# Local attention and a two-matrix FFN on one core: the stationary of the FFN matmuls read with a step of four columns

## The chip, the cores and the metric

The kernel runs on one core of a Trainium2 chip. Its time is the time of one execution on the device, in microseconds (us); several executions are made and their median is given. The core's engines are TensorE (PE in the profile, with its loads of the stationary shown apart as PEld), VectorE (DVE), ScalarE (ACT), GpSimd (POOL) and SyncE (SP). In this kernel SP issues every transfer between DRAM and the chip's memory. A matmul on PE has a stationary operand, which is loaded by an instruction of its own, and a moving operand, which is streamed against it.

## The reference

The input is q, k and v for 4 batches of 8 heads, 768 tokens, 64 numbers per head, and 8 memory keys and values per head. Attention is local: tokens go in chunks of 32, and a chunk sees the memory, 16 tokens to its left, itself, and 8 to its right.

```python
for c in range(S // 32):
    k_full = concat([mem_k, k[:, :, max(0, 32*c - 16) : min(S, 32*c + 40)]])   # v_full likewise
    scores = q[:, :, 32*c : 32*c + 32] @ k_full.T / sqrt(64)
    a = exp(scores - max(scores)); a = a / (sum(a) + 1e-9)
    out[:, :, 32*c : 32*c + 32] = a @ v_full
x = out as 3072 tokens x 512
h = x @ w_in                                # 512 -> 2048
g = where(h >= 1, h, where(h <= -1, 0, (h + 1)**2 / 4))
result = g @ w_out                          # 2048 -> 512
```

## The kernel before

The 3072 tokens are six blocks of `TB = 512` tokens (`NB = 6`), and the FFN's 2048 hidden numbers are `NFC = 16` slices of 128. A step `s` is one slice `fc` of one block `blk`. In each step PE makes the hidden slice and then, two steps later (`LAG`), adds its share of the output. Both weights and both activations are split into a high and a low part (`wh`, `wl`; `xh`, `xl`; `gh`, `gl`) of type fp32r, and three of the four products are summed.

*Hidden product* (`pe_hidden`, and the same lines in `early_step`). The stationary is a 128-column piece of the weight slice, one for each of the `NP = 4` groups of 128 input channels; the moving operand is x, 512 tokens wide. The weight slice of one `fc` lies in a partition as 512 words, group after group, so piece `cc` is the 128 words from `cc * P`. Three products by four groups are 12 matmuls.

*Output product* (`pe_products`). Here the stationary is a piece of the gated activation, 128 tokens, and the moving operand is the row of w_out, 512 columns wide. A block has `NT = 4` token tiles, tile `t` being the 128 tokens from `t * P`. Three products by four tiles are again 12 matmuls. Their sums stay in PSUM over all 16 slices (`acc`), one bank for a tile.

*Gating*. ACT and DVE turn the hidden slice into `gh` and `gl`. *Store*: after the last slice of a block each tile's sum is copied by DVE or ACT and written by SP into 128 consecutive rows of `out`, one row (2 KB) per partition.

*The beginning.* Blocks 0 and 1 are done by the list `FIRST`, an order written out by hand in which each name is one piece of work: `g` and `n` are attention, `w` the decoding of a weight transfer by DVE and ACT, `A`, `B`, `C`, `D` are FFN steps over half a block (256 tokens, two token tiles; A and B the halves of block 0, C and D those of block 1, slices 0 to 3 each), and `J`, `E` are FFN steps over the whole of block 0 or 1. A half step's hidden matmuls have 256 moving columns. In it `pe_products` gets two tiles only, and `g` is the half's own 256 tokens.

*The rest.* From `s = first * NFC` with `first = 2` on, a loop runs the steps of blocks 2 to 5, with the attention of later blocks spread between them. All instructions are kept in the program's order on each engine.

The weights come in 16 transfers of 1 MB, packed in 64 bits per weight, in the order that `weight_order` gives; `_lay_out` arranges all inputs before the program runs.

Of the kernel before, what the change touches and what calls it, by code (L numbers as in the profile page):

```python
# [16 lines left out]
P = 128  # L17
CHUNK, LEFT, RIGHT = 32, 16, 8
TB = 512
NCH = TB // CHUNK  # L20
NT = TB // P
# [47 lines left out]
def attn_ffn_kernel(ctx: ExitStack, tc: tile.TileContext, first_qk, first_v, qk, vw, w, out):  # L69
    nc = tc.nc  # L70
    engines = (nc.tensor, nc.scalar, nc.vector, nc.gpsimd, nc.sync)
    pe, act, dve, pool, sp = (InOrder(tc, e) for e in engines)
    NP = first_qk.shape[0]
# [3 lines left out]
    DM = NP * P  # L77
    NPW = w.shape[0]
    NFC = NPW
# [14 lines left out]
    def two_banks(tag, name):  # L94
        return ps_2.tile([P, 2, 512], F32, name=name, tag=tag)
# [43 lines left out]
    def weights(which, fc, part):  # L139
        i, j = place[which, fc]  # L140
        c0 = part * n2 + j * DM
        return ws[i][:, c0 : c0 + DM]
# [248 lines left out]
    gate, gs, acc, hidden = {}, {}, {}, {}  # L391

    def hidden_terms(wh, wl, xh, xl):
        return [(m, x, cc) for m, x in ((wh, xh), (wl, xh), (wh, xl)) for cc in range(NP)]

    def pe_products(outs, gh, gl, wh, wl, fc):

        kinds = list(enumerate(((gh, wh), (gh, wl), (gl, wh))))
        todo = [(t, kind) for kind in kinds for t in range(len(outs))]
        if fc == NFC - 1:  # L400
            todo.sort(key=lambda x: x[0])
        for t, (i, (g, m)) in todo:
            ts = slice(t * P, (t + 1) * P)
            pe.matmul(outs[t], g[:, ts], m, start=fc == 0 and i == 0, stop=fc == NFC - 1 and i == 2)

    def pe_hidden(s):
        blk, fc = divmod(s, NFC)
        xh, xl = xts[blk]
        hp = hidden[s] = ps_h.tile([P, 512], F32, name="ps_h")
        wh, wl = weights(0, fc, 0), weights(0, fc, 1)  # L410
        terms = hidden_terms(wh, wl, xh, xl)
        for n, (m, x, cc) in enumerate(terms):
            pe.matmul(hp, m[:, cc * P : (cc + 1) * P], x[:, cc], start=n == 0, stop=n == len(terms) - 1)

    def gating(s):

# [24 lines left out]
    def pe_out(s):  # L441
        blk, fc = divmod(s, NFC)
        gh, gl = gs.pop(s)
        if fc == 0:
            pairs = [two_banks(f"a{i}", "ps_o") for i in range(NT // 2)]
            acc[blk] = [pairs[t // 2][:, t % 2] for t in range(NT)]
        wh, wl = weights(1, fc, 0), weights(1, fc, 1)
        pe_products(acc[blk], gh, gl, wh, wl, fc)

    items, halves = [], []  # L450

    def early_step(name, blk, tokens, fc):

        items.append(name)
        size = len(tokens) * P
        xh, xl = (x[:, :, tokens[0] * P : tokens[0] * P + size] for x in xts[blk])
        n = 0
        if size < TB:
            n = len(halves) % 2
            halves.append(name)  # L460
        hp = ps_h.tile([P, 512], F32, name="ps_h")[:, 0:size]
        wh, wl = weights(0, fc, 0), weights(0, fc, 1)
        terms = hidden_terms(wh, wl, xh, xl)
        for i, (m, x, cc) in enumerate(terms):
            pe.matmul(hp, m[:, cc * P : (cc + 1) * P], x[:, cc], start=i == 0, stop=i == len(terms) - 1)
        yield
        if n == 0:
            tiles = (
                gpool.tile([P, TB], F32, name="gw", tag="gw"),
                gpool.tile([P, TB], F32, name="gt"),  # L470
                gpool.tile([P, TB], F32R, name="gh", bufs=3),
                gpool.tile([P, TB], F32R, name="gl", bufs=3),
            )
            if size < TB:
                both["g"] = tiles
        else:
            tiles = both["g"]
        g, t, gh, gl = (x[:, n * HT : n * HT + size] for x in tiles)
        act.activation(g, hp, AF.Relu, bias=0.5, scale=0.5)
        act.activation(t, hp, AF.Relu, bias=-1.0)  # L480
        act.activation(g, g, AF.Square)
        yield
        dve.scalar_tensor_tensor(g, g, 1.0, t, op0=ALU.min, op1=ALU.add)
        yield
        act.copy(gh, g)
        yield
        dve.tensor_tensor(gl, g, gh.bitcast(F32), op=ALU.subtract)
        yield
        if fc == 0:
            acc.setdefault(blk, [None] * NT)  # L490
            pair = two_banks(f"a{tokens[0] // 2}", "ps_o")
            for t in tokens:
                acc[blk][t] = pair[:, t % 2]
        wh, wl = weights(1, fc, 0), weights(1, fc, 1)
        pe_products([acc[blk][t] for t in tokens], gh, gl, wh, wl, fc)
        yield
        if fc < NFC - 1:
            return
        for t in tokens:
            if t % 2 == 0:  # L500
                ob = apool.tile([P, 2, DM], F32, name="ob", tag="f", bufs=2)
            (act.copy if t % 2 else dve.tensor_copy)(ob[:, t % 2], acc[blk][t])
            r0 = blk * TB + t * P
            sp.dma_start(out[r0 : r0 + P, :], ob[:, t % 2])
            yield

    def store(blk):
        for t in range(NT):
            src = acc[blk][t]
            if t % 2 == 0:  # L510
                ob = apool.tile([P, 2, DM], F32, name="ob", tag="f", bufs=2)
            dst = ob[:, t % 2]
            if t == NT - 1:
                dve.tensor_copy(dst[:, 0 : DM // 2], src[:, 0 : DM // 2])
                act.copy(dst[:, DM // 2 : DM], src[:, DM // 2 : DM])
            elif t % 2:
                act.copy(dst, src)
            else:
                dve.tensor_copy(dst, src)
            r0 = blk * TB + t * P  # L520
            sp.dma_start(out[r0 : r0 + P, :], dst)

    def keep_warm(n):

# [27 lines left out]
    for name in FIRST.split():  # L552
# [4 lines left out]
        if name not in chains:  # L557
            kind, i = name[0], int(name[1:])
# [2 lines left out]


    begin = {}
    first = 2
    for blk in range(first + 1, NB):
        for half in range(2):
            begin[(blk - 1) * NFC + STARTS[half]] = (blk, half)
# [6 lines left out]
    for s in range(first * NFC, steps):  # L574
# [30 lines left out]
        else:  # L605
            n, i = LAST // LAG, s - first * NFC
# [6 lines left out]
    for s in range(steps - LAG, steps):  # L613
        pe_out(s)
    store(NB - 1)


def weight_order(n):

    order = [(0, 0), (0, 1)]  # L620
    for fc in range(2, n):
        order += [(0, fc), (1, fc - 2)]
    return order + [(1, n - 2), (1, n - 1)]
# [5 lines left out]
def _lay_out(q, k, v, mem_k, mem_v, moe_w_in, moe_w_out):  # L629
    import numpy as _np  # L630

    B, H, S, D = q.shape
    NM, NC = mem_k.shape[2], S // CHUNK
    NP, W = H // 2, NM + LEFT + CHUNK + RIGHT
    NB = B * S // TB

    def windows(mem, a):

        pad = _np.pad(a, ((0, 0), (0, 0), (LEFT, RIGHT), (0, 0)))
        win = [  # L640
            _np.concatenate([mem, pad[:, :, c * CHUNK : (c + 1) * CHUNK + LEFT + RIGHT]], axis=2)
            for c in range(NC)
        ]
        return _np.stack(win, axis=1).reshape(B * NC, H, W, D)

    def transposed(a):

        return a.transpose(1, 3, 0, 2).reshape(NP, 2 * D, -1)


    qt = transposed(q).reshape(NP, 2 * D, NB * 2, TB // 2).transpose(2, 1, 0, 3)
    kw = windows(mem_k, k).reshape(NB * 2, NCH // 4, 2, NP, 2, 2, W // 2, D)

    k0 = kw.transpose(0, 4, 7, 3, 1, 2, 5, 6).reshape(NB * 2, 2 * D, NP, NCH // 2 * W)
    kw = _np.stack([kw[:, :, 0], kw[:, :, 1][..., ::-1, :, :]], axis=2)
    kw = kw.transpose(0, 4, 7, 3, 1, 2, 5, 6).reshape(NB * 2, 2 * D, NP, NCH // 2 * W)
    qk0 = _np.concatenate([qt, k0], axis=3)[0:2].reshape(2, 2 * D, 2, -1).transpose(0, 2, 1, 3)
    qk = _np.concatenate([qt, kw], axis=3).reshape(NB, 2, 2 * D, -1)[1:]
    vw = windows(mem_v, v).reshape(NB, NT, 4, NP, 2, W, D)

    v0 = vw[0].reshape(2, 2, 4, NP // 2, 2, 2, W, D).transpose(0, 3, 1, 6, 4, 2, 5, 7)

    v1 = vw[1:].reshape(NB - 1, 2, NT // 2, 2, 2, NP, 2, W, D).transpose(0, 1, 3, 7, 5, 2, 4, 6, 8)
    DM, DF = moe_w_in.shape
    n = DF // 128

    slices = (
        moe_w_in.reshape(DM // 128, 128, n, 128).transpose(2, 1, 0, 3).reshape(n, 128, DM),
        moe_w_out.reshape(n, 128, DM),
    )  # L670
    w = _np.stack([slices[which][fc] for which, fc in weight_order(n)])
    w = w.reshape(n, 2, 128, DM).transpose(0, 2, 1, 3).reshape(n, 128, 2 * DM)
    arrays = {

        "first_qk": qk0.reshape(NP, 2 * D, -1),
        "first_v": v0.reshape(NP, 2 * W, NCH * D),
        "qk": qk,
        "vw": v1.reshape(NB - 1, 2, 2 * W, -1),
        "w": _np.ascontiguousarray(w).view(_np.int64),
    }  # L680
    return {name: _np.ascontiguousarray(a) for name, a in arrays.items()}
# [23 lines left out]
```

## Time and profile before

| | |
|---|---|
| median of 3 executions | 599.97 us (599.84 to 600.01) |
| the profiled execution | 600.11 us |
| its span, first to last instruction | 598.3 us |
| granted TensorE clock, mean | 0.999 |
| instructions | 12265 |
| PE busy, share of the span | 582.7 us, 97%, 5496 matmuls |
| loads of the stationary (PEld) | 483.5 us, 81%, 5496 loads |
| DVE, ACT | 325.6 us (54%), 280.3 us (47%) |
| weights | 16 transfers of 1024 KB |
| stores | 24 of 256 KB, 2.0 us from issue to landing |

The profile is of one execution. A row of a timeline gives the start, the time until the last of its instructions ended, the engine, the source line, the operation with the tiles that it writes and reads, the shape and the number of instructions. Since every operation is recorded through one helper (`InOrder`), nearly all rows carry line 63, and the tiles tell them apart: `ps_h` is the hidden product, `ps_o` the output product, `ps_s` and `ps_x` the two products of attention; `xth` and `xtl` are the parts of x, `wr` the decoded weights, `gh` and `gl` the gated activation. A row of a group gives the number of instructions, their busy time, the mean duration of one in ns, and the time for which the engine was idle just before them with what ended it. A row of a window gives for each engine the busy time and the number of instructions in that stretch, then the granted clock, the share of the transfer engines' time, and GB/s.

### The profile page before, as it was taken

The numbers are of one execution on the slowest core, as the hardware profiler recorded it, in microseconds if no ns is written. First come the engines' busy times: TensorE is split into PE (matmuls) and PEld (weight loads), VectorE is DVE, ScalarE is ACT, GpSimd is POOL, SyncE is SP. The second block draws the span as 40 slices with busy tenths as digits, with TensorE's granted clock in tenths as the row PEclk, the third lists the DMA queues.
The fourth block names the chain that finished last, engine by engine and source line by source line (L and its number), as shares of the span: only waits on it lengthen the run. The fifth ranks groups of instructions, "written<-read, shape, count | busy, mean of one in ns | idle before, by whom it ended". The sixth has DMA issues, their size and how long they took to land.

```text
span 598.3 us, 12265 instructions
## 1 busy us (share of the span) xinstructions
PE 582.7 (97%) x5496; PEld 483.5 (81%) x5496; DVE 325.6 (54%) x466; ACT 280.3 (47%) x503; POOL 0.7 (0%) x6
## 2 busy tenths in 40 slices
PE   5899999999999999999999999999999999999996
PEld 2888888788888888888888888888888888888885
DVE  5999999986474224636423644623564632322222
ACT  2689864554435335444435443434443444543442
POOL 0000000000000000000000000000000000000000
PEclk9999999999999999999999999999999999999999
DMA  8999300424051004012101223200310000100001
GB/s 355 422 418 419 148 1 0 178 82 168 1 177 71 0 1 158 26 65 108 71 1 71 107 71 107 71 1 34 144 71 2 1 2 0 71 0 1 0 1 70
DMA packets 9844, 55.31 MB, mean 92 GB/s; under 512 B 1088, under 2 KB 1088, under 8 KB 5184
## 3 DMA queue, kind: packets, MB, share of 16 engines
q1 hardware_dynamic: 9792, 54.53, 23.6%
q8 instruction: 43, 0.70, 0.5%
q14 instruction: 9, 0.07, 0.0%
HBM read 48.23 MB, written 6.29 MB: 91 GB/s over the span
## 4 chain that ended last, share of the span: by engine, by line
PE 82%; DVE 15%; issue 2%; DMA 1%; ACT 0%; DVEq 0%; ACTq 0%
PE ps_o L63 38%; PE ps_h L63 38%; DVE f L63 6%; PE ps_x L63 3%; DVE wr L63 2%; PE ps_s L63 2%; DVE gw L63 1%; DVE gl L63 1%; DVE pr L63 1%; DVE den L63 1%; DMA qk<-in_first_qk_dram 1%; DVE pt L63 1%; DVE mx L63 1%; DVE xtl L63 0%; DVE rin L63 0%
## 5 line engine op out<-in xcount | busy, mean ns | idle before, releaser
L63 PE MATMUL ps_h<-xth,wr 128*128 128x512 f32 (+1 forms) x832 | 195.6, 377 | 1.1 <-DVE wr L63 1.1
L63 PE MATMUL ps_o<-wr,gh 128*128 128x512 f32 x768 | 194.7, 390 | 0.0
L63 PEld LDWEIGHTS ps_h<-xth,wr 128*128 128x128 f32 x832 | 149.0, 190 | 30.3 <-DVE wr L63 1.5
L63 PEld LDWEIGHTS ps_o<-wr,gh 128*128 128x128 f32 x768 | 143.3, 188 | 29.4
L63 DVE SCALAR_TENSOR_TENSOR gw<-gw,gt 128x512 f32<-128x512 f32 (+1 forms) x104 | 67.2, 649 | 164.9 <-ACT gw L63 164.6
L63 ACT ACTIVATE gw<-ps_h 128x512 f32<-128x512 f32 (+1 forms) x104 | 58.6, 563 | 159.0 <-PE ps_h L63 158.9
L63 PE MATMUL ps_o<-wr,gl 128*128 128x512 f32 x384 | 106.9, 389 | 0.0
L63 PE MATMUL ps_h<-xtl,wr 128*128 128x512 f32 (+1 forms) x416 | 104.8, 374 | 0.0
L63 DVE TENSOR_TENSOR gl<-gw,gh 128x512 fp32r<-128x512 f32 (+1 forms) x104 | 67.4, 649 | 65.8 <-ACT gh L63 65.7
L63 ACT CAST gh<-gw 128x512 fp32r<-128x512 f32 (+1 forms) x104 | 61.1, 590 | 69.9 <-DVE gw L63 69.9
L63 PEld LDWEIGHTS ps_h<-xtl,wr 128*128 128x128 f32 x416 | 75.3, 190 | 13.9
L63 PEld LDWEIGHTS ps_o<-wr,gl 128*128 128x128 f32 x384 | 72.1, 188 | 15.1
L63 ACT ACTIVATE gw<-gw 128x512 f32<-128x512 f32 (+1 forms) x104 | 62.4, 600 | 0.0
L63 ACT ACTIVATE gt<-ps_h 128x512 f32<-128x512 f32 (+1 forms) x104 | 58.3, 561 | 0.0
L63 DVE STREAM_TRANSPOSE pt<-pr 32x512 f32<-32x512 f32 (+1 forms) x60 | 41.2, 698 | 1.3
L63 DVE SCALAR_TENSOR_TENSOR f<-w,f 128x1024 uint32<-128x1024 uint32 x32 | 39.0, 1220 | 0.4
L63 ACT ACTIVATE pr<-pr 128x1024 f32<-128x1024 f32 (+1 forms) x14 | 13.1, 937 | 35.1 <-DVE pr L63 35.0
L63 PEld LDWEIGHTS ps_x<-pt,v 64*64 64x64 f32 x1536 | 25.1, 142 | 5.0 <-issue 3.3
L63 PE MATMUL ps_x<-pt,v 64*64 64x32 f32 x1536 | 26.6, 226 | 1.2 <-ACT pt L63 1.2
L63 ACT CAST xth<-ps_x 128x512 fp32r<-128x512 f32 x24 | 13.1, 591 | 20.6 <-PE ps_x L63 20.6
L63 ACT CAST wr<-f 128x1024 fp32r<-128x1024 f32 x16 | 16.8, 1051 | 11.7 <-DVE f L63 11.7
L63 PEld LDWEIGHTS ps_s<-qk 64*32 64x32 f32 x1536 | 17.1, 112 | 6.1 <-issue 3.1
(27 smaller groups left out, 182.6 us busy)
## 6 DMA issues: line engine op xcount, KB each, us to landing
w<-in_w_dram SPq DMA_DIRECT2D x16, 1024.0 KB, 19.8
qk<-in_qk_dram SPq DMA_DIRECT2D x10, 1536.0 KB, 6.5
v<-in_vw_dram SPq DMA_DIRECT2D x10, 1024.0 KB, 5.5
out_dram<-ob SPq DMA_DIRECT2D x24, 256.0 KB, 2.0
qk<-in_first_qk_dram SPq DMA_DIRECT2D x4, 768.0 KB, 8.7
v<-in_first_v_dram SPq DMA_DIRECT2D x4, 512.0 KB, 12.7
```

The lines of the kernel that those rows point to most:

```text
L63: return self.tc.keep_in_program_order(getattr(self.engine, name)(*args, **kwargs))
```

## The change

The stationary of both FFN products is read with a step. For the hidden product the words of a weight slice are laid out interleaved: word `4 * j + cc` of a partition is column `j` of group `cc`, and the piece for group `cc` is every fourth word. For the output product a token tile is every fourth token of its block (blocks 2 to 5), or every second token of its half block (blocks 0 and 1, whose early steps work on halves). A store writes the rows of `out` that belong to such a tile. The operands of each matmul of the hidden product are the same numbers as before; those of the output product are other groups of 128 tokens, with the same results for each token.

```diff
+    first = 2
+
+    def of_tile(blk, t):
+        n = NT // 2 if blk < first else NT
+        at = t // n * n * P + t % n
+        return slice(at, at + (P - 1) * n + 1, n)
+
+    def rows_of(blk, t):
+        return out[blk * TB : (blk + 1) * TB, :][of_tile(blk, t), :]
+
-    def pe_products(outs, gh, gl, wh, wl, fc):
+    def pe_products(outs, gh, gl, wh, wl, blk, fc):
...
-            ts = slice(t * P, (t + 1) * P)
-            pe.matmul(outs[t], g[:, ts], m, start=fc == 0 and i == 0, stop=fc == NFC - 1 and i == 2)
+            pe.matmul(outs[t], g[:, of_tile(blk, t)], m, start=fc == 0 and i == 0, stop=fc == NFC - 1 and i == 2)
...  (pe_hidden, and the same in early_step)
-            pe.matmul(hp, m[:, cc * P : (cc + 1) * P], x[:, cc], start=n == 0, stop=n == len(terms) - 1)
+            pe.matmul(hp, m[:, cc::NP], x[:, cc], start=n == 0, stop=n == len(terms) - 1)
...  (early_step; the same in store)
-            r0 = blk * TB + t * P
-            sp.dma_start(out[r0 : r0 + P, :], ob[:, t % 2])
+            sp.dma_start(rows_of(blk, t), ob[:, t % 2])
...  (_lay_out)
-        moe_w_in.reshape(DM // 128, 128, n, 128).transpose(2, 1, 0, 3).reshape(n, 128, DM),
+        moe_w_in.reshape(DM // 128, 128, n, 128).transpose(2, 1, 3, 0).reshape(n, 128, DM),
```

More of the change, by code (lines that the diff above doesn't have):

```diff
@@ L447, in pe_out @@
         wh, wl = weights(1, fc, 0), weights(1, fc, 1)
-        pe_products(acc[blk], gh, gl, wh, wl, fc)
+        pe_products(acc[blk], gh, gl, wh, wl, blk, fc)
     items, halves = [], []
@@ L464, in early_step @@
         for i, (m, x, cc) in enumerate(terms):
-            pe.matmul(hp, m[:, cc * P : (cc + 1) * P], x[:, cc], start=i == 0, stop=i == len(terms) - 1)
+            pe.matmul(hp, m[:, cc::NP], x[:, cc], start=i == 0, stop=i == len(terms) - 1)
         yield
@@ L494, in early_step @@
         wh, wl = weights(1, fc, 0), weights(1, fc, 1)
-        pe_products([acc[blk][t] for t in tokens], gh, gl, wh, wl, fc)
+        pe_products([acc[blk][t] for t in tokens], gh, gl, wh, wl, blk, fc)
         yield
@@ L519, in store @@
                 dve.tensor_copy(dst, src)
-            r0 = blk * TB + t * P
-            sp.dma_start(out[r0 : r0 + P, :], dst)
+            sp.dma_start(rows_of(blk, t), dst)
     def keep_warm(n):
@@ L563, in attn_ffn_kernel @@
     begin = {}
-    first = 2
     for blk in range(first + 1, NB):
```

## The prediction

> **What bounds the kernel now.** I read the page first: the busy line, the slices and the engines' shares of the chain that ended last.
>
> ```profile
> span 598.3 us, 12265 instructions
> PE 582.7 (97%) x5496; PEld 483.5 (81%) x5496; DVE 325.6 (54%) x466; ACT 280.3 (47%) x503; POOL 0.7 (0%) x6
> PE   5899999999999999999999999999999999999996
> DVE  5999999986474224636423644623564632322222
> PEclk9999999999999999999999999999999999999999
> PE 82%; DVE 15%; issue 2%; DMA 1%; ACT 0%; DVEq 0%; ACTq 0%
> ```
>
> TensorE (PE) carries the chain. VectorE (DVE) is full only in the first eight slices, some 110 us, where it decodes weights; afterwards it has room. The granted clock is full. A matmul's end in this trace is modelled, so a PE that is 97% busy can still have room. I therefore take start times from the timeline: first a step in the middle (24 matmuls of 512 moving columns, each with a stationary of its own), then a stretch with 256 moving columns, then the four transposes of an attention group (once a narrow view of the first, once all four).
>
> ```profile
> 300.33 1.77 PEld L63 LDWEIGHTS ps_h<-xth,wr 128*128 128x128 f32 x8
> 300.56 1.98 PE L63 MATMUL ps_h<-xth,wr 128*128 128x512 f32 x8
> 303.28 1.98 PE L63 MATMUL ps_o<-wr,gh 128*128 128x512 f32 x8
> ...
> 118.91 1.12 PE L63 MATMUL ps_h<-xth,wr 128*128 128x256 f32 x8
> 120.34 2.00 PE L63 MATMUL ps_o<-wr,gh 128*128 128x512 f32 x8
> ...
> 30.95 0.27 PE L63 MATMUL ps_h<-ident,pr 128*128 128x128 f32 x1
> 30.95 0.60 PE L63 MATMUL ps_h<-ident,pr 128*128 128x128 f32 x4
> ```
>
> From 300.56 to 303.28 lie twelve matmuls (eight of the high and four of the low part of x): 2.72 us / 12 = 227 ns each. From 118.91 to 120.34 lie twelve of 256 columns: 1.43 us / 12 = 119 ns each. The transposes: (0.60 - 0.27) / 3 = 110 ns from start to start. The first two differ by 108 ns for 256 columns, 0.42 ns a column, with 12 ns fixed: both follow the moving operand. At that pace 128 moving columns would take 66 ns. The transposes take 110, so something else limits them, and what is left there is the load of a 128-column stationary. **A load therefore holds its path for at most 110 ns**, although its own record is longer:
>
> ```profile
> L63 PEld LDWEIGHTS ps_h<-xth,wr 128*128 128x128 f32 x832 | 149.0, 190 | 30.3 <-DVE wr L63 1.5 <-issue 0.2
> L63 PEld LDWEIGHTS ps_o<-wr,gh 128*128 128x128 f32 x768 | 143.3, 188 | 29.4
> L63 PEld LDWEIGHTS ps_o<-wr,gl 128*128 128x128 f32 x384 | 72.1, 188 | 15.1
> L63 PEld LDWEIGHTS ps_h<-xtl,wr 128*128 128x128 f32 x416 | 75.3, 190 | 13.9
> 36.62 1.03 PEld L63 LDWEIGHTS ps_h<-xth,wr 128*128 128x128 f32 x8
> ```
>
> The last row has eight loads of 190 ns (1.52 us) in 1.03 us: records of following loads overlap, so 190 ns is a latency with a part that isn't occupancy. And the load of the next stationary runs beside the matmul before it: the row at 300.33 begins 0.23 us ahead of its matmuls. So there are two kinds of place. Under 512 moving columns a load may grow from 110 to about 227 ns, by a factor of 2.06, before anyone waits. Under 256 columns it has 119, 9 ns more than now.
>
> **The change part by part.** No instruction is added or removed. What changes is the address step of the stationary's columns, the order of the words in w_in and the rows of `out` that a store writes.
>
> Counts. Loads of the hidden product: 832 + 416 = 1248, all with a step of four (16 bytes of a partition). Loads of the output product: 768 + 384 = 1152; blocks 0 and 1 have 2 x 16 x 12 = 384 of them, with a step of two, and blocks 2 to 5 the other 768, with a step of four. Step four in all: 2016. Those of them that stand before a 256-column matmul are the half-token steps A, B, C and D:
>
> ```profile
> L63 PE MATMUL ps_h<-xth,wr 128*128 128x256 f32 x128 | 19.4, 297 | 0.0
> L63 PE MATMUL ps_h<-xtl,wr 128*128 128x256 f32 x64 | 10.7, 291 | 0.0
> 113.00:150.00 37.00, 37.00 (x484) 32.67 (x472) 29.88 (x47) 17.78 (x44) 0.00 (x0) 1.00 0.40 144
> 20.00:105.00 85.00, 82.15 (x817) 70.26 (x818) 84.13 (x113) 61.40 (x105) 0.00 (x0) 1.00 0.54 223
> 105.00:107.00 2.00, 1.05 (x4) 0.53 (x4) 2.00 (x2) 1.70 (x4) 0.00 (x0) 1.00 0.43 102
> ```
>
> 128 + 64 = 192, half of them (C and D, block 1) after 113 us, where PE is busy 37.00 of 37.00 us: any nanosecond there is on the path. The other half (A and B) lies in the first 50 us, where DVE has 84.13 of 85 us and PE still waits 2.85 us in this stretch and 0.95 us at 105; some of a delay there is swallowed, some pushes DVE, which waits for hidden results in its own order. I count half of it as exposed, 0 to all as the range. So 96 + 48 = 144 loads count (96 to 192).
>
> What a stepped load costs isn't in this trace: every PE operand in it is contiguous. The bounds come from the nearest rows.
>
> ```profile
> L63 DVE TENSOR_SCALAR f<-w 128x1024 uint32<-128x1024 uint32 x16 | 11.0, 687 | 0.0
> L63 DVE TENSOR_TENSOR gl<-gw,gh 128x512 fp32r<-128x512 f32 x88 | 60.8, 691 | 64.8 <-ACT gh L63 64.8
> L63 DVE TENSOR_TENSOR gl<-gw,gh 128x256 fp32r<-128x256 f32 x16 | 6.6, 418 | 1.0 <-ACT gh L63 0.9
> ```
>
> - Below: 110 ns, unchanged. A gain is excluded: under 512 and 256 columns the moving operand sets the pace, so a faster load would bring nothing.
> - DVE's decode reads every second word, 1024 words over 8192 bytes of a partition, in 687 ns with its fixed part, that is 16 bytes in 1.34 ns. It is quicker per word than the contiguous two-operand row (691 - 418 = 273 ns for 256 words), so nothing of a step shows in it. A load of step four has to walk 128 x 16 = 2048 bytes: at this pace 172 ns; without the fixed part (about 145 ns by the two rows of `gl`) 136 ns.
> - Above: PE's own moving operand walks 2048 contiguous bytes in 227 ns at most. A load that walked no faster would take 227 ns.
>
> All of these are at or under 227 ns, so in every 512-column step the longer load stays beside the matmul; the cover is the 227 ns itself, and past that each ns costs 1 ns on 2016 - 192 = 1824 loads, 1.8 us. Under 256 columns the cost per ns above 119 is 0.144 us (0.096 to 0.192): at 136 ns 2.4 us, at 172 ns 7.6 us, at 227 ns 15.6 us (10.4 to 20.7).
>
> I take the unchanged 110 ns, cost 0. It is the value of the load itself, and the only row with a stepped read shows no price for it; the load asks for one word per 0.85 ns, which is a slower demand than DVE's two words per 1.06 ns in that row.
>
> The Trainium skill speaks against this. Its page "SBUF — State Buffer", section "Specifications (TRN2)", gives lines of 16 bytes and wants at least two hits per line for full bandwidth; a step of four 4-byte words has one, a step of two has two. It names no price for a load; by it the 1248 + 768 loads of step four would get slower and the 384 of step two not, and the time would be that of the first rival below. DVE's row has two hits per line and agrees with the rule; no run here has shown one hit per line.
>
> The stores: 24 of 256 KB, as before one row of `out` (2 KB) per partition, only that rows that follow in a tile are four (blocks 0 and 1: two) apart in DRAM. The same pieces, so I take nothing; only the last four lie on the path, at the end:
>
> ```profile
> out_dram<-ob SPq DMA_DIRECT2D x24, 256.0 KB, 2.0
> 593.10 2.47 SPq L63 DMA_DIRECT2D out_dram<-ob  x4
> ```
>
> Bounds: their landing could move by some tenths of the 2.0 us, +-0.5 us. SP's queue holds the same issues in the same order; what waits behind a store there is the next block's loads, many us ahead of need. The x tiles, gating and attention are untouched, and w_in is rearranged outside the program, with the same 16 transfers.
>
> Sum: 0 under 512 columns, 0 under 256, 0 at the stores. The profiled execution took 600.11 us (span 598.3), 0.14 above the median of 599.97; so the forecast is 600.0.
>
> **The rivals.**
> 1. The stepped load gets slower, but not beyond 227 ns. Place: the 256-column steps alone. It decides from 119 ns on. For it: only 9 ns of room there, and PE without a gap after 113 us. Against: DVE's row. Taken at 172 ns, 600.0 + 7.6 = 607.6 us; from 601.6 (136 ns, C and D alone) to 620.7.
> 2. The load goes past 227 ns, or the two reads of PE get into each other's way by as much. It decides from a factor of 2.06. Against: no row near gives so slow a walk. Price 1.8 us per ns under 512 columns: at three times 110 ns, 330, it is 103 x 1.8 = 185 us, and 211 x 0.144 = 30 under 256: about 815 us.
> 3. The four stores of a block now interleave in DRAM. If the program orders them as overlapping, each waits for the landing of the one before: at the end, issues 2.0 us apart from 593.10, the fourth landing at 601.1 in place of about 597.2 (last issue 593.10 + 2.47 less its record of some 0.3, plus 2.0): +3.9, 603.9 us. Against: the rows are disjoint. For: their ranges are not.
> 4. Something outside this sum makes it faster, by placement or landing: 599.
>
> **How the numbers follow.** Chances: forecast 0.50; rival 1 0.33; rival 2 0.10; rival 3 0.04; rival 4 0.03. About 0.2% (1.2 us) is what a measurement of this kernel can tell from no change. The forecast gives "within" with 0.50; rivals 1 to 3 are slower by more than 0.2%, 0.47 in all; rival 4 gives faster, 0.03. Range: down to 599.2 for the landing of the stores; up to 614.0, which takes in rival 1 to a load of about 216 ns by the 144 count, and rival 3. Left out are rivals 2 and 4 and the top of rival 1, about 0.18. The likeliest alone has 599.4 to 600.6.
>
> **What would show it.** The four load groups in the costliest groups tell the step's own price: records near 190 mean no price, longer ones with the same start distances mean a hidden one. The distance of the 256-column starts is the judge: 119 ns for the forecast, 136 and more for rival 1, with the step at 113 us and the end later by the sum. The middle steps must keep 227 ns; more is rival 2. The loads of the output product in blocks 0 and 1 (step two) against those later (step four) show whether it is the step's width that counts. The last four stores must issue within 2.5 us; 2 us apart is rival 3. The forecast fails if the path of the load, unlike DVE's, can't take a new 16 bytes for every column at its pace.

## The result: 6.1% slower

The changed kernel takes 636.65 us (median of 4 executions, 636.53 to 636.73) against 599.95 us before: 36.7 us more, a ratio of 1.0612 with a 95% interval of 1.0593 to 1.063. The forecast was no change, with a range up to 614.0.

The page of the changed kernel, in the lines that answer to those of before:

```profile
span 634.9 us, 12265 instructions
PE 620.2 (98%) x5496; PEld 594.1 (94%) x5496; DVE 327.2 (52%) x466; ACT 281.6 (44%) x503; POOL 0.7 (0%) x6
PE   5899999999999999999999999999999999999996
PEclk9999999999999999999999999999999999999999
PE 96%; DVE 2%; DMA 1%; ACT 0%; issue 0%; DVEq 0%; ACTq 0%
L63 PEld LDWEIGHTS ps_h<-xth,wr 128*128 128x128 f32 x832 | 203.6, 313 | 2.6 <-issue 0.2
L63 PEld LDWEIGHTS ps_o<-wr,gh 128*128 128x128 f32 x768 | 175.0, 271 | 8.4
L63 PEld LDWEIGHTS ps_h<-xtl,wr 128*128 128x128 f32 x416 | 106.1, 313 | 0.0
L63 PEld LDWEIGHTS ps_o<-wr,gl 128*128 128x128 f32 x384 | 90.8, 271 | 5.1
out_dram<-ob SPq DMA_DIRECT2D x24, 256.0 KB, 2.2
```

The instructions are the same in number and the clock is full. DVE and ACT have the same work as before. What moved is PEld, 483.5 to 594.1 us: the mean load record of the hidden product went from 190 to 313 ns, that of the output product, a third of which has a step of two, from 188 to 271. PE, which had only 82% of the chain, now has 96%: DVE's 15% in the first 110 us is down to 2%, because PE has become the slower one there too. The timeline of a step in the middle and of a stretch with 256 moving columns, as in the prediction, and of an output product of block 0 (its step is two):

```profile
301.22 2.04 PE L63 MATMUL ps_h<-xth,wr 128*128 128x512 f32 x8
304.04 2.04 PE L63 MATMUL ps_o<-wr,gh 128*128 128x512 f32 x8
306.86 0.40 PE L63 MATMUL ps_h<-xth,wr 128*128 128x512 f32 x1
...
128.88 1.92 PE L63 MATMUL ps_h<-xth,wr 128*128 128x256 f32 x8
130.63 1.09 PE L63 MATMUL ps_h<-xtl,wr 128*128 128x256 f32 x4
131.57 2.02 PE L63 MATMUL ps_o<-wr,gh 128*128 128x512 f32 x8
...
71.44 2.03 PE L63 MATMUL ps_o<-wr,gh 128*128 128x512 f32 x8
73.30 1.10 PE L63 MATMUL ps_o<-wr,gl 128*128 128x512 f32 x4
```

Under 512 columns a step of 24 matmuls takes 306.86 - 301.22 = 5.64 us, 235 ns each, where it was 227. Under 256 columns the four matmuls of the low part take 0.94 us, 235 ns each (the most frequent distance in the trace is 233), where it was 119. And in block 0, with a step of two, eight starts take 1.86 us, 233 ns each. **So nearly every matmul of the FFN now starts 231 to 240 ns after the one before it, whether 256 or 512 columns stream.** The price by these distances: 192 x 113 ns (233 against 120, the most frequent distances in the two traces) = 21.7 us under 256 columns, 1824 x 8.2 = 15.0 us under 512 with a step of four, 384 x 6 = 2.3 us with a step of two. That is 39.0, and 36.7 were measured. Laid start against start, the two traces show the difference under 256 columns: what follows a 512-column matmul of the FFN grew by 17.3 us in all, as in the sum, but what follows a 256-column one by 19.3, of which 9.1 lie in the first 107 us. Before the change fifteen of those early starts already stood 213 ns apart, for a reason that the profile doesn't show, so they lost only 20 ns each:

```profile
25.73 1.05 PE L63 MATMUL ps_h<-xtl,wr 128*128 128x256 f32 x4
26.58 1.35 PE L63 MATMUL ps_h<-xth,wr 128*128 128x256 f32 x8
```

The last four stores of the changed kernel stand as before:

```profile
629.46 2.52 SPq L63 DMA_DIRECT2D out_dram<-ob  x4
```

### The profile page after: what moved, and what is told of

Read it like the earlier page. It is cut to its first block, busy times and chain, and to the rows that moved or that the text cites. A ratio compares the mean times of both kernels' runs of the same rounds, so it can differ in the third digit from the quotient of the medians.

```text
span 634.9 us, 12265 instructions
## 1 busy us (share of the span) xinstructions
PE 620.2 (98%) x5496; PEld 594.1 (94%) x5496; DVE 327.2 (52%) x466; ACT 281.6 (44%) x503; POOL 0.7 (0%) x6
## 4 chain that ended last, share of the span: by engine, by line
PE 96%; DVE 2%; DMA 1%; ACT 0%; issue 0%; DVEq 0%; ACTq 0%
PE ps_h L63 47%; PE ps_o L63 43%; PE ps_x L63 3%; PE ps_s L63 3%; DMA qk<-in_first_qk_dram 1%; DVE f L63 1%; DVE pr L63 1%; DVE den L63 0%; DVE mx L63 0%; DVE wr L63 0%; DVE ob L63 0%; ACT gw L63 0%; DVE rin L63 0%; ACT pr L63 0%; ACT pt L63 0%
## 5 line engine op out<-in xcount | busy, mean ns | idle before, releaser
L63 PE MATMUL ps_h<-xth,wr 128*128 128x512 f32 (+1 forms) x832 | 214.9, 401 | 0.0
L63 PEld LDWEIGHTS ps_h<-xth,wr 128*128 128x128 f32 x832 | 203.6, 313 | 2.6 <-issue 0.2
L63 PE MATMUL ps_o<-wr,gh 128*128 128x512 f32 x768 | 200.3, 397 | 0.0
L63 PEld LDWEIGHTS ps_o<-wr,gh 128*128 128x128 f32 x768 | 175.0, 271 | 8.4
L63 PE MATMUL ps_h<-xtl,wr 128*128 128x512 f32 (+1 forms) x416 | 114.5, 397 | 0.0
L63 PE MATMUL ps_o<-wr,gl 128*128 128x512 f32 x384 | 109.9, 397 | 0.0
L63 PEld LDWEIGHTS ps_h<-xtl,wr 128*128 128x128 f32 x416 | 106.1, 313 | 0.0
L63 PEld LDWEIGHTS ps_o<-wr,gl 128*128 128x128 f32 x384 | 90.8, 271 | 5.1
L63 PE MATMUL ps_s<-qk 64*32 64x64 f32 x1536 | 19.5, 239 | 1.1 <-DMA qk<-in_first_qk_dram 1.1
```

What stands on the lines that cost most here:

```text
L63: return self.tc.keep_in_program_order(getattr(self.engine, name)(*args, **kwargs))
```

## The experiments

The theory after this result: a load of step four holds its own path for 233 ns. Rival A: the two reads of TensorE, stationary and moving, get into each other's way. Rival B: the output side costs, tiles or stores. The rows of PE shown below are from stretches in which the granted clock was 1.00, except where it is said.

**One half of the change at a time.** The first kernel has only this:

```diff
-            pe.matmul(hp, m[:, cc * P : (cc + 1) * P], x[:, cc], ...)
+            pe.matmul(hp, m[:, cc::NP], x[:, cc], ...)           # and w_in interleaved as in the change
```

> Only the hidden product's stationary has the step of four; token tiles and rows of out are contiguous. Theory (the load's own pace): a load of step four holds its path some 233 ns, whatever runs beside it, so 192 starts under 256 columns go from 120 to 233 ns (+21.7 us, some 2 us of it swallowed early) and 1056 under 512 columns from 227 to 235 (+8.4): about 628 us, ps_o starts stay at 227 ns. Rival A (the two reads of TensorE get into each other's way): a load beside a shorter stream is hindered for less time, so the loss per matmul should be smaller under 256 columns than what makes 233: below 615 us. Rival B (the cost sits in the output side, tiles or stores): within 1 us of 600.

Measured: 629.29 us, a ratio of 1.0492 (1.0473 to 1.051). The timeline:

```profile
131.62 1.09 PE L63 MATMUL ps_h<-xtl,wr 128*128 128x256 f32 x4
132.55 2.01 PE L63 MATMUL ps_o<-wr,gh 128*128 128x512 f32 x8
...
300.58 2.04 PE L63 MATMUL ps_h<-xth,wr 128*128 128x512 f32 x8
303.40 1.99 PE L63 MATMUL ps_o<-wr,gh 128*128 128x512 f32 x8
306.13 1.10 PE L63 MATMUL ps_h<-xth,wr 128*128 128x512 f32 x4
```

Four hidden matmuls of 256 columns take 0.93 us, 233 ns each; twelve of 512 columns 2.82 us, 235 each; the twelve of the output product, whose stationary is contiguous here, 2.73 us, 227 each. The loss stays with the stepped stationary and hardly spreads to its neighbours. Both rivals fall short.

The second has the other half: `g[:, of_tile(blk, t)]` and `rows_of` as in the change, hidden product and w_in as before.

> Only the output product's stationary is stepped (two in blocks 0 and 1, four in blocks 2 to 5), with the stores' rows that belong to it; the hidden product is as before. Theory: 768 starts from 227 to 235 ns (+6.1) and 384 of step two from 227 to 233 (+2.3): 608.4 us. With the hidden part alone this adds up to the whole change. Rival B (stores): more than 612 us, with the excess at the ends of blocks. Rival C (a price for step two needs the stepped hidden loads beside it): the 384 stay at 227 ns, 606 us.

Measured: 608.55 us, 1.0141 (1.0125 to 1.0156). The two halves alone add up to 29.3 + 8.6 = 37.9 us, and the whole change costs 36.7.

```profile
62.08 2.03 PE L63 MATMUL ps_o<-wr,gh 128*128 128x512 f32 x8
63.95 1.09 PE L63 MATMUL ps_o<-wr,gl 128*128 128x512 f32 x4
...
300.29 2.04 PE L63 MATMUL ps_o<-wr,gh 128*128 128x512 f32 x8
303.11 1.99 PE L63 MATMUL ps_h<-xth,wr 128*128 128x512 f32 x8
```

In block 0, with a step of two, eight starts take 1.87 us, 234 ns each; in block 2, with a step of four, twelve take 2.82 us, 235 each. The price of step two is there without any stepped hidden load (rival C falls).

The third keeps `rows_of` alone; the matmuls read `g[:, t * P : (t + 1) * P]` as before.

> The stores write rows of out that are four (two) apart, but the matmuls read contiguous stationaries as before, so that tokens land in other rows: only the transfers differ. Theory: 600.0 us, last four stores within 2.5 us of each other, landing 2.0 to 2.2 us. Rival B: up to 604 us, stores at the end 2 us apart.

Measured: 600.12 us, 1.0003 (0.9993 to 1.0013). The four last stores issue within one row of 2.47 us, as before; landing has a median of 2.3 us. The stores cost nothing.

**The width of the step.** Four kernels change only the hidden stationary. Step two, with w_in interleaved by pairs of groups:

```diff
-  m[:, cc * P : (cc + 1) * P]
+  m[:, cc // 2 * 2 * P + cc % 2 : (cc // 2 + 1) * 2 * P : 2]
```

> Only the hidden product is stepped, with a step of two (groups interleaved by pairs). Theory (two words of every 16 bytes are nearly enough): load records near 193 ns, starts under 256 columns about 126 ns and under 512 about 233, 1248 x 6 ns = 7.5: 607.5 us. Rival C (that 6 ns is not the step's): 600.0 us, 120 and 227 ns. Rival D (price in proportion to the step, a third of step four's): a load of about 151 ns, starts under 256 columns 151 ns (+6 us), under 512 unchanged at 227: 606 us.

Measured: 606.05 us, 1.0099 (1.0084 to 1.0114). The load records have a mean of 195 ns.

```profile
119.81 0.64 PE L63 MATMUL ps_h<-xtl,wr 128*128 128x256 f32 x4
120.28 2.00 PE L63 MATMUL ps_o<-wr,gh 128*128 128x512 f32 x8
...
302.52 2.03 PE L63 MATMUL ps_h<-xth,wr 128*128 128x512 f32 x8
305.32 1.98 PE L63 MATMUL ps_o<-wr,gh 128*128 128x512 f32 x8
```

Under 256 columns 0.47 / 4 = 118 ns, as before the change; under 512 columns 2.80 / 12 = 233 ns. So 1056 x 6.3 ns = 6.7 us, where 6.1 were measured, and nothing under 256 columns: the 6 ns per load that the theory put on all 1248 is a price of the 512-column matmuls alone. Rival D, in proportion, has the right time and is out by the distances; rival C is out by the time and by the distance under 512 columns.

Step three, out of the contiguous slice (`m[:, cc : cc + 127 * 3 + 1 : 3]`), and step eight, over two neighbouring slices of a transfer (`m[:, cc::8]` of a 1024-word part):

> Hidden stationary read with a step of three words (12 bytes) out of the contiguous slice; the four groups read overlapping words, so the hidden numbers are others. Of every four words read, two lie in one piece of 16 bytes and two alone in theirs. Theory P (a word alone in its 16 bytes costs double, two together nothing): a load of 110 x 1.5 = 165 to 175 ns, starts under 256 columns at that, under 512 at 233 as with step two: 606 + 192 x 0.052 = 615 us. Theory Q (a threshold: any step under 16 bytes is like two): 606 us, 120 ns. Theory R (price in proportion to the bytes walked): nothing at step two in the 256-column starts speaks against it already; 192 ns, 619 us.

> Hidden stationary read with a step of eight words (32 bytes) over two neighbouring slices; the hidden numbers are others. Theory P and Q (what counts is that each word has 16 bytes to itself): as at step four, 629 us, 233 ns under 256 and 235 under 512 columns. Theory R (bytes walked): twice the walk, loads near 460 ns, which 1248 matmuls wait for: about 890 us.

Measured: 615.72 us at step three, 1.0261 (1.0217 to 1.0305), and 640.84 at step eight, 1.068 (1.0625 to 1.0734). The four low-part matmuls of 256 columns, first of step three (with twelve of 512 columns), then of step eight:

```profile
123.94 0.87 PE L63 MATMUL ps_h<-xtl,wr 128*128 128x256 f32 x4
124.64 2.02 PE L63 MATMUL ps_o<-wr,gh 128*128 128x512 f32 x8
...
306.10 2.03 PE L63 MATMUL ps_h<-xth,wr 128*128 128x512 f32 x8
308.90 1.98 PE L63 MATMUL ps_o<-wr,gh 128*128 128x512 f32 x8
```

```profile
133.13 1.13 PE L63 MATMUL ps_h<-xtl,wr 128*128 128x256 f32 x4
134.09 2.02 PE L63 MATMUL ps_o<-wr,gh 128*128 128x512 f32 x8
```

0.70 / 4 = 175 ns and 0.96 / 4 = 240 ns (over the whole traces the median is 177 at step three, and the most frequent distance 243 at step eight). Step three falls near where theory P had it: two words in common 16 bytes go together, a word alone counts double. A threshold at 16 bytes (Q: 120 ns at step three) misses by far, and so do the bytes walked (R: 192 ns at step three, 460 at step eight). Step eight costs 10 ns per load more than step four, and the kernel 12 us more than P's 629, which P did not foresee; twice the walk would have cost over 200 ns. Under 512 columns step three takes 2.80 / 12 = 233 ns, though its load of 177 ns is far shorter than the stream: the same 6 ns as at step two.

**The load by itself.** In block 2 each hidden matmul is cut into four of 128 moving columns, each with its own load; once contiguous, once at step four:

```diff
-            pe.matmul(hp, m[:, ...], x[:, cc], ...)
+        cuts = range(0, TB, P) if blk == 2 else (0,)
+        width = TB // len(cuts)
+        for c in cuts:
...
+                pe.matmul(hp[:, c : c + width], m[:, ...], x[:, cc, c : c + width], ...)
```

> The kernel before, but in block 2 alone each hidden matmul of 512 moving columns is cut into four of 128, each with its own load of the same contiguous stationary: 16 x 48 loads in place of 16 x 12. Nothing but the load can set a pace above 66 ns there. Theory: 110 ns from start to start, so 600 + 16 x (48 x 0.110 - 12 x 0.227) = 641 us. If a load of this type takes less, down to 66 ns: 607 us; if the 120 ns under 256 columns was already the load's, 120 ns and 649 us.

> The same cut in block 2, with the hidden product's stationary at a step of four. Theory (the load's own pace, whatever streams beside it): 233 ns from start to start as under 256 columns, 629.3 + 16 x (48 x 0.233 - 12 x 0.235) = 763 us. Rival A (the two reads hinder each other): only 54 ns of each load run beside a stream, so the load should be clearly under 233 ns; at 170 ns 715 us.

Measured, one execution each: 643.04 and 788.5 us. The starts, contiguous:

```profile
234.17 1.06 PE L63 MATMUL ps_h<-xth,wr 128*128 128x128 f32 x8
235.06 0.61 PE L63 MATMUL ps_h<-xtl,wr 128*128 128x128 f32 x4
```

and at step four, with two windows of the same run:

```profile
304.33 2.03 PE L63 MATMUL ps_h<-xth,wr 128*128 128x128 f32 x8
306.20 1.10 PE L63 MATMUL ps_h<-xtl,wr 128*128 128x128 f32 x4
```

```profile
220.00:240.00 20.00, 20.00 (x89) 18.45 (x88) 5.41 (x8) 7.29 (x13) 0.00 (x0) 1.00 0.00 1
240.00:280.00 40.00, 40.00 (x159) 38.15 (x160) 4.06 (x6) 5.92 (x11) 0.00 (x0) 0.66 0.07 27
```

0.89 / 8 = 111 ns for a contiguous load, 1.87 / 8 = 234 for one of step four. Under 128 moving columns or under 256, it is the same 233: the load's own pace, not a collision (rival A). The 25 us above the 763 expected are the clock: from 240 us on, where this cut begins, the granted clock falls to a mean of 0.66 to 0.70 (the starts at step four above are from this stretch), and 132 starts of 512-column output matmuls between the cuts go from 227 to 427 ns, 26 us in all. The 233 ns do not move with that clock: the median is 234 ns where it was granted in full and 233 where half was granted.

**Where the 6 ns under 512 columns sit.** The hidden matmuls of blocks 2, 3 and 4 are cut into 384 + 128, 448 + 64 and 320 + 192 columns, at steps one, two and four.

> The kernel before, with the 512 moving columns of the hidden product cut in two: 384 + 128 in block 2, 448 + 64 in block 3, 320 + 192 in block 4, each piece with its own load. Control for the next two: starts at the larger of a load's 111 ns and width / 2.4 + 13 ns, so 173, 200 and 147 ns for the wide pieces and 111 for the narrow ones: 600 + 192 x (57 + 84 + 31) ns = 633 us.

> The same cuts with a hidden step of two, to place the 6 ns that a step of two costs under 512 columns and not under 256. Theory W (it is there whenever the stream is clearly longer than the load): 179, 206 and 153 ns for 384, 448 and 320 columns, 640 us. Theory X (it belongs to the full 512 columns): 173, 200 and 147 ns as in the control, 637 us. The narrow pieces show the load itself at step two: 111 to 116 ns.

> The same cuts with a hidden step of four. Theory (a load of 233 ns sets the pace wherever the stream is shorter): 233 ns from start to start for every width from 64 to 448, 629.3 + 3 x 192 x (2 x 233 - 235) ns = 762 us. If the load got longer beside a longer stream, starts would grow with the width, from 233 at 64 to more at 448.

Measured, one execution each: 635.26, 641.01 and 784.47 us. The low-part matmuls of 448 columns, at step one and then at step two:

```profile
388.91 0.97 PE L63 MATMUL ps_h<-xtl,wr 128*128 128x448 f32 x4
389.72 0.97 PE L63 MATMUL ps_h<-xth,wr 128*128 128x64 f32 x8
```

```profile
383.21 0.97 PE L63 MATMUL ps_h<-xtl,wr 128*128 128x448 f32 x4
384.03 1.01 PE L63 MATMUL ps_h<-xth,wr 128*128 128x64 f32 x8
```

0.81 / 4 = 202 ns and 0.82 / 4 = 205. Over the whole traces the medians at step two against step one are 149 to 146 ns (320 columns), 173 to 174 (384), 205 to 202 (448) and 233 to 227 (512); the narrow pieces, which show the load, 118 to 112 (64 columns). So the load of step two is itself some 6 ns longer, still far inside any stream, and the price beside a stream reaches 6 ns only at the full 512 columns. That speaks for X rather than W, but not cleanly, and the time doesn't decide: of the 5.8 us above the control, 576 narrow pieces at 6 ns make 3.5, which neither theory had in its sum. Why 512 columns pay it stays open. At step four every width from 64 to 384 has a median of 233 to 235, 448 has 238, most of it between 229 and 243: the load does not grow clearly with the stream beside it. The 784 us against 762 come from the granted clock again, which was near 0.9 from 260 to 540 us (121 starts of output matmuls at 427 ns).

**The row on which the prediction leaned.** DVE's first decode instruction, cut in two (with the numbers put in for the names):

```diff
-        dve.tensor_scalar(f, u, 3, None, op0=ALU.logical_shift_left)
+        dve.tensor_scalar(f[:, 0:514], u[:, 0:514], 3, ...)                       # step two
+        dve.tensor_scalar(f[:, 514:1024], raw[i][:, 3 : 3 + 4 * 509 + 1 : 4], 3, ...)   # step four
```

> The kernel before, with DVE's first decode instruction cut in two: 514 words at a step of two as before, and 510 at a step of four (other words, so the low halves of the weights differ). It measures the row from which the prediction took that a step costs nothing. Theory P carried over to DVE: 417 ns for the first (145 fixed + 514 x 0.53) and for the second twice the pace, 685 ns. If DVE has no such price: 415 ns for both. The time rises by some 16 x (0.15 to 0.4) us, 602 to 606 us.

Measured, one execution: 606.29 us. The groups by shape:

```profile
L63 DVE TENSOR_SCALAR f<-w 128x510 uint32<-128x510 uint32 x16 | 10.1, 630 | 0.0
L63 DVE TENSOR_SCALAR f<-w 128x514 uint32<-128x514 uint32 x16 | 6.9, 429 | 0.0
```

510 words at step four take 630 ns, 514 at step two 429. DVE pays for step four as well, about 0.4 ns a word, less than the 685 ns of twice the pace; the row of before could not show it, because at step two every 16 bytes serve two words.

## Why the prediction was wrong

**What held.** The bound and its places were read rightly: PE's start distances, a load of at most 110 ns (111 by itself), 119 ns of cover under 256 columns, 192 loads with 9 ns of room, PE without a gap after 113 us. That the stores and their rows cost nothing held too (600.12 us alone), and the sums by these distances came out: with 233 ns put in, the halves were expected at 628 and 608.4 us and measured at 629.29 and 608.55.

**The step that failed** is the price of one load, "I take the unchanged 110 ns, cost 0". It was taken from DVE's decode row, as "the only row with a stepped read shows no price". But that row has a step of two. With the load at 111, 118, 177, 233 and 243 ns for steps of one, two, three, four and eight, step two is nearly free and step four is not, and the same DVE instruction, run at a step of four, takes half as long again. A row is near only if it has what is feared; here that was a word alone in its 16 bytes, and no row of before had one.

**The upper bound failed too**, by 6 ns: "a load that walked no faster would take 227 ns" counted bytes of contiguous data. The load is not slowed by bytes walked (step eight walks twice as far for 10 ns more) but by words that stand alone. The same figures can be read by pieces of 16 bytes: steps two, three, four and eight touch 64, 96, 128 and 128 of them, which is 1.84, 1.84, 1.82 and 1.90 ns for each piece. This reading, an estimate that no run tests apart, gives step two's 118 ns as well, while a contiguous load touches 32 pieces and has another limit. The load of step four takes 233 ns, past the 227 at which rival 2 was said to decide.

**A third step failed: "0 under 512 columns"** for any load shorter than the stream. With loads of 118 and 177 ns (steps two and three) 512-column matmuls already start 233 ns apart in place of 227, and step two alone made the kernel 6.1 us slower. If these 6 ns are there at step four too, they are about 13 of the 36.7 us (on 1824 + 384 matmuls); their cause is open.

By the prediction's own prices a load of 233 ns would give (233 - 119) x 0.144 = 16.4 us under 256 columns and 6 x 1.8 = 11 us under 512, 27 us in all. What lacks to 36.7 are two sizes: the count of 144 was too low, since PE became the slower engine before 113 us too and nearly all of the 192 were paid (19.3 us); and a 512-column matmul loses 8 ns rather than 6, and 6 even at step two, where the load is short.

**The rivals.** Rival 1 named the mechanism and the place of just over half of the loss and had the range end too early (227 ns, 620.7 us); rival 2 named the threshold and took three times 110 ns as its example, where 2.1 times came. Rivals 3 and 4 did not occur. The rule of the Trainium skill that spoke against the change ("SBUF — State Buffer", section "Specifications (TRN2)", two hits per 16-byte line) sorts all five steps rightly: 111 ns with four hits, 118 with two, 177 with two of four words alone, 233 and 243 with one hit. The runs agree with it. The price, which the page does not give, is a factor of two in the load's pace: (233 - 111) / 128 = 0.95 ns more for each column that stands alone.

Of the 8 ns under 512 columns at step four, one can't say how they divide: the load's 233 ns alone would force six of them, and the 6 ns seen at steps two and three would be there without it. That the load counts shows at step eight, where a load of 243 ns goes with distances of mostly 242 to 249 ns under 512 columns.

## What to carry to other kernels

A stationary of 4-byte words loads almost as fast with a step of two (118 ns in place of 111 for 128 columns), though under 512 moving columns each matmul here still lost 6 ns; from the step on at which each word has 16 bytes to itself, the load takes twice as long, 233 ns. A load longer than the stream can't be hidden, so look for the matmuls with the fewest moving columns first: here 192 of 2400 carried more than half of the loss. And when a trace lacks the operation, ask of the nearest row not only whether it is alike, but whether it contains the very thing that could cost; if it doesn't, it bounds nothing.

## What the runs showed that was not expected

- A load's record says little of its occupancy: 190 ns recorded for 111 ns of pace, 313 for 233. The start distances under a narrow moving operand tell it.
- A step of two or three costs a 512-column matmul about 6 ns (227 to 233), while under 256 and 384 columns step two cost nothing. The cause is open.
- PE whose rows stand back to back can still lose its clock: with 128 columns streamed for every load of 233 ns, the granted clock fell from 1.00 to a mean of 0.66 to 0.70, and the loads kept their 233 ns.
